# Token transform of batches 2 to 8: nine products become seven, and one table holds the issue order

## The chip, the cores and the metric

The kernel runs on one core of one Trainium2 chip. The metric is device time in microseconds (us). The kernel before takes 995.22 us, the median of three runs (994.12 to 995.35). The engines are PE (TensorE), DVE (VectorE), ACT (ScalarE), POOL (GpSimd) and SP (SyncE, here only an issuer of DMAs).

## The reference, cut to what matters

```
kv  = einsum('bhsd,bhse->bhde', k, v)          # 8 batches, 8 heads, 576 tokens, 64 wide
out = einsum('bhsd,bhde->bhse', q, kv)
x   = out / sqrt(mean(out*out, -1) + 1e-6) * g_norm   # then heads side by side: (8, 576, 512)
u   = x + real(fft(fft(x, axis=1), axis=2))
un  = (u - mean(u)) / sqrt(var(u) + 1e-6)
y   = u + relu(un @ w_ch1) @ w_ch2              # 512 -> 2048 -> 512
```

The Fourier transform over the 576 tokens is the "token transform" of the title; the one over the 512 channels is the "channel transform". Both are matrix products with cosine and sine tables.

## The kernel before, in words

The work is a list of small operations (`op`, `dma`), each with an engine, a cost, a rank, what it comes after and the buffers it holds. In the kernel before, `Plan.go` plays this list through on assumed costs and so finds an order; `MOVES` changes ranks, `SHIFTS` moves single operations in the finished line, and `settle` applies that. Every engine then executes its own instructions in the order in which they were emitted, and waits in place for what an instruction needs. SP's DMAs too are issued strictly in that order.

The code counts batches from 0, so "batches 2 to 8" are b = 1 to 7. For each batch: `plan_kv` (k'v, tile ps_k), `plan_q` (q transposed, ps_q), `plan_out` (q times kv, ps_o), `plan_y` (the root mean square), `plan_fold`, `plan_seq` (the token transform), `plan_chn` (the channel transform and the sum u), `plan_turn` (u transposed, split in two parts, into the blocks unTh and unTl for the feed-forward part). A product of two float32 matrices is made of three products of parts, high x high, high x low, low x high (`passes`), since each operand is kept as a high part and a low rest.

Fold and token transform: the symmetric halves of the 576 tokens are folded, which leaves 289 rows in three tiles t = 0, 1, 2 with 97, 96 and 96 rows. `plan_fold` makes the high part `xh` (ACT) and the rest `xl` (POOL or DVE) of each tile; in b = 1 to 7 the tiles come in the order 0, 1, 2. `plan_seq` then has four groups per batch (cosine or sine part, and two halves of the channels); a group sums nine products into one bank ps_f: three tiles times three passes, each 128 x 290 with 96 or 97 rows summed over (line 1532; b = 0 uses line 1544). The tables sit in `cs`, high and low, for three tiles. `p0_mm` (line 1964) does the same nine products once more for a single column of all batches.

The feed-forward part: NA = 3 of the 16 slices of the hidden layer are computed for a block of 512 tokens as soon as it is turned ("early", tiles ps_h and acc, lines 1012 and 1029), between the operations of the batches that follow. The remaining slices come after all batches. Line 1084 (`ps_s <- still`) emits products of a constant with itself whose result nobody reads ("spare" products); the plan puts them where PE has nothing ready.

What orders the work around the change: PE's and SP's own queues, in the emitted order; a fold needs `plan_y`'s result, a group of the token transform needs all three tiles' `xl`.

Of the kernel before, what the change touches and what calls it, by code (L numbers as in the profile page):

```python
# [9 lines left out]
F32 = mybir.dt.float32  # L10
# [4 lines left out]
ALU = mybir.AluOpType  # L15
# [61 lines left out]
SHIFTS = [  # L77
    ("plan_spare.go/PE/-/-", 20, 0),
    ("plan_w.<lambda>/DVE/w1/2", 3, -1),
    ("plan_w.<lambda>/DVE/w1/1", 1, -2),  # L80
    ("plan_q.take/ACT/3/11", 0, 2),
    ("plan_spare.go/PE/-/-", 18, 0),
    ("plan_spare.go/PE/-/-", 26, 0),
    ("plan_w.<lambda>/DVE/w2/2", 1, -4),
    ("plan_first_out.mean/DVE/0/1", 0, -2),
    ("plan_chn.<lambda>/DVE/1/1", 1, -6),
    ("plan_spare.go/PE/-/-", 31, 0),
    ("plan_first_out.square/ACT/0/2", 1, 9),
    ("plan_chn.<lambda>/ACT/1/2", 0, 5),
    ("plan_fold.even.go/DVE/1/1", 1, -2),  # L90
    ("plan_fold.fold/DVE/1/0", 0, -6),
    ("plan_spare.go/PE/-/-", 16, 0),
    ("plan_kv.<lambda>/POOL/2/-", 1, 9),
    ("plan_kv.<lambda>/POOL/5/-", 1, -2),
    ("plan_seq.<lambda>/PE/0/1", 0, -1),
    ("plan_turn.high/ACT/0/0", 0, -2),
    ("plan_out.red/DVE/2/1", 1, 10),
    ("plan_seq.<lambda>/PE/0/0", 1, 2),
    ("plan_q_load.load/SP/1/02", 0, 10),
    ("plan_spare.go/PE/-/-", 9, -4),  # L100
    ("plan_fold.mul/DVE/2/0", 0, -4),
    ("plan_q_load.<lambda>/SP/3/-", 0, 1),
    ("plan_spare.go/PE/-/-", 27, 0),
    ("plan_out.<lambda>/ACT/2/1", 0, -1),
    ("plan_kv.<lambda>/DVE/0/-", 0, 9),
    ("plan_fold.zero/ACT/1/1", 0, 4),
    ("plan_out.<lambda>/ACT/2/1", 1, 1),
    ("plan_first.<lambda>/PE/e0/-", 9, 3),
    ("plan_chn.put.<lambda>/SP/0/0", 1, 2),
    ("plan_kv.<lambda>/SP/1/-", 8, 1),  # L110
    ("plan_fold.zero/ACT/2/2", 0, -1),
    ("plan_chn.mix/DVE/0/0", 1, 5),
    ("plan_y.last/DVE/2/-", 0, -1),
    ("plan_seq.<lambda>/PE/0/0", 0, -2),
    ("plan_out.<lambda>/ACT/1/0", 1, 4),
    ("plan_kv.go/PE/1/-", 1, 1),
    ("plan_w.<lambda>/ACT/w2/0", 0, 9),
    ("plan_first.<lambda>/PE/e0/-", 4, 1),
    ("plan_first_out.mean/DVE/0/2", 0, 1),
    ("plan_first_out.mul/DVE/0/1", 0, 1),  # L120
    ("plan_early.<lambda>/ACT/e0/-", 3, -4),
    ("plan_out.scale/POOL/1/2", 0, 8),
    ("plan_chn.<lambda>/DVE/0/0", 0, 1),
    ("plan_kv.<lambda>/SP/5/-", 8, -2),
# [12 lines left out]
    ("plan_early.<lambda>/PE/e0/-", 10, -1),
    ("plan_out.scale/POOL/2/1", 1, 1),
    ("plan_spare.go/PE/-/-", 22, 0),
    ("plan_first_out.red/DVE/0/2", 1, -6),  # L140
    ("plan_fold.zero/ACT/1/2", 0, -2),
    ("plan_q.take/ACT/3/11", 0, -9),
    ("plan_w.<lambda>/DVE/w2/1", 1, 6),
    ("plan_first_out.red/DVE/0/2", 0, 1),
    ("plan_w.<lambda>/DVE/w2/0", 0, 9),
    ("plan_kv.<lambda>/SP/5/-", 7, 7),
    ("plan_w.<lambda>/DVE/w2/1", 0, 8),
    ("plan_first.<lambda>/DVE/e0/-", 1, -1),
    ("plan_spare.go/PE/-/-", 34, 0),
    ("plan_spare.go/PE/-/-", 33, 1),  # L150
    ("plan_chn.<lambda>/ACT/0/1", 0, 3),
    ("plan_q.turn/PE/4/01", 0, 9),
    ("plan_turn.turn/PE/0/1", 0, -2),
    ("plan_q.take/ACT/0/01", 0, -7),
    ("plan_chn.mm/PE/1/0", 1, 4),
    ("plan_turn.high/ACT/0/2", 1, -2),
    ("plan_chn.put.<lambda>/SP/0/0", 1, -2),
    ("plan_q_load.load/SP/1/-", 0, -1),
    ("plan_y.root/ACT/1/-", 0, 3),
    ("plan_w.<lambda>/DVE/w2/1", 5, -6),  # L160
    ("plan_spare.go/PE/-/-", 19, 0),
    ("plan_turn.low/DVE/0/1", 2, -1),
    ("plan_first.<lambda>/PE/e0/-", 0, -2),
    ("plan_turn.high/ACT/4/0", 2, 4),
    ("plan_out.red/DVE/2/1", 1, -3),
    ("plan_kv.<lambda>/POOL/3/-", 0, 1),
    ("plan_kv.<lambda>/ACT/6/-", 0, -2),
    ("plan_q.turn/PE/7/02", 0, 1),
    ("plan_chn.add_r/POOL/5/1", 0, -1),
    ("plan_early.<lambda>/ACT/e1/-", 7, 1),  # L170
    ("plan_y.recip/DVE/4/-", 0, -2),
    ("plan_early.<lambda>/ACT/e2/-", 5, -3),
    ("plan_fold.<lambda>/ACT/2/0", 0, -4),
    ("plan_turn.low/DVE/1/2", 0, 3),
    ("plan_out.red/DVE/6/2", 0, 1),
    ("plan_q.take/ACT/7/10", 0, 1),
    ("plan_first.<lambda>/PE/e2/-", 3, -1),
    ("plan_kv.<lambda>/SP/3/-", 9, -3),
    ("plan_out.mm/PE/3/2", 0, 6),
    ("plan_out.scale/POOL/4/2", 0, -3),  # L180
    ("plan_fold.<lambda>/ACT/3/1", 0, 9),
    ("plan_out.mm/PE/4/0", 0, 1),
    ("plan_chn.<lambda>/DVE/2/2", 1, 2),
    ("plan_chn.<lambda>/DVE/4/0", 0, 4),
    ("plan_first.<lambda>/PE/e3/-", 11, -6),
    ("plan_early.<lambda>/PE/e1/-", 7, -1),
    ("plan_early.<lambda>/ACT/e3/-", 3, -3),
    ("plan_out.og/ACT/6/1", 0, -7),
    ("plan_q.take/ACT/4/11", 0, -10),
    ("plan_turn.turn/PE/1/1", 0, 2),  # L190
    ("plan_seq.mm/PE/3/3", 0, 3),
    ("plan_chn.add_l/POOL/5/1", 0, 1),
    ("plan_seq.low/DVE/3/1", 0, -1),
    ("plan_q_load.load/SP/3/-", 0, 4),
    ("plan_kv.<lambda>/SP/4/-", 4, 2),
    ("plan_early.<lambda>/ACT/e1/-", 3, 1),
    ("plan_chn.<lambda>/DVE/0/0", 1, 9),
    ("plan_seq.mm/PE/3/0", 0, 2),
    ("plan_seq.mm/PE/3/2", 0, 3),
    ("plan_fold.<lambda>/ACT/3/1", 0, 4),  # L200
    ("plan_first.<lambda>/ACT/e3/-", 1, -1),
    ("plan_fold.low/DVE/1/1", 0, -1),
    ("plan_seq.<lambda>/ACT/2/1", 0, -2),
    ("plan_q.take/ACT/2/11", 0, -3),
    ("plan_turn.high/ACT/2/0", 3, 2),
    ("plan_turn.high/ACT/3/0", 3, 1),
    ("plan_chn.add_r/POOL/5/1", 0, -1),
    ("plan_out.<lambda>/ACT/6/0", 0, -2),
    ("plan_fold.<lambda>/ACT/1/1", 0, -4),
    ("plan_fold.low/DVE/2/2", 0, -2),  # L210
    ("plan_turn.low/DVE/1/1", 2, -1),
    ("plan_chn.<lambda>/DVE/3/2", 0, -3),
    ("plan_first.<lambda>/ACT/e2/-", 2, -2),
    ("plan_y.last/DVE/2/-", 0, -3),
    ("plan_kv.<lambda>/POOL/4/-", 1, 3),
    ("plan_seq.mm/PE/5/0", 0, 1),
    ("plan_turn.low/DVE/3/2", 0, -1),
    ("plan_out.og/ACT/5/2", 1, 3),
    ("plan_fold.<lambda>/ACT/1/1", 0, -2),
    ("plan_first.<lambda>/ACT/e2/-", 0, -1),  # L220
    ("plan_chn.mm/PE/5/2", 1, 2),
    ("plan_chn.mm/PE/5/2", 0, -4),
    ("plan_kv.go/PE/5/-", 1, -1),
    ("plan_turn.low/DVE/1/2", 2, -1),
    ("plan_turn.turn/PE/1/0", 1, 1),
    ("plan_chn.<lambda>/DVE/2/1", 0, 4),
    ("plan_fold.even.go/POOL/4/1", 1, -4),
    ("plan_fold.even.go/POOL/2/1", 1, -6),
    ("plan_fold.<lambda>/ACT/3/1", 0, -1),
    ("plan_out.red/DVE/4/1", 0, 6),  # L230
    ("plan_chn.mm/PE/3/0", 1, 9),
    ("plan_kv.<lambda>/POOL/4/-", 1, -2),
# [2292 lines left out]
```

## Time and profile before

| | |
|---|---|
| median of three timed runs | 995.22 us (994.12 to 995.35) |
| span of the profiled execution, first to last instruction | 993.5 us (its own device time is not listed apart from the span) |
| PE busy | 982.3 us, 99% |
| DVE, ACT, POOL busy | 690.1, 363.4, 397.6 us |
| DMA moved | 166.06 MB |
| PE in the first 60 us | 53.87 us busy |
| PE from 60 to 560 us | 499.9 us busy of 500 |

The profile counts an instruction as busy from its start to its modelled end. Neighbouring matmuls overlap, so the duration of one (some 300 to 400 ns) is longer than its share of PE's time; that share is read from a row of the chain of waits, where a merged piece gives the time of a whole run of products.

### The profile page before, as it was taken

The page shows a single profiled execution, that of the slowest core. Times are in us where ns is not written, and L with a number is a line of the kernel's source. Part 1 is how long each engine was busy: PE and PEld are TensorE (multiplying, and loading weights), DVE is VectorE, ACT ScalarE, POOL GpSimd, SP SyncE. Part 2 cuts the span into 40 slices and gives each one's busy share as a digit, 9 for nine tenths or more (in the row PEclk, how much of TensorE's full clock was granted, in tenths as well). Part 3 has the DMA queues.
Part 4 walks back from the last instruction along what each step waited for, and adds up shares of the span by engine and source line. Part 5 has one row for each costly group of instructions (what it writes and reads, how often), then busy time and mean ns, then how long its engine had stood idle before and what let it go on. Part 6 is the DMA issues. An engine that isn't in the chain of part 4 may idle for free.

```text
span 993.5 us, 17707 instructions
## 1 busy us (share of the span) xinstructions
PE 982.3 (99%) x6838; PEld 858.5 (86%) x6838; DVE 690.1 (69%) x1365; ACT 363.4 (37%) x731; POOL 397.6 (40%) x391
## 2 busy tenths in 40 slices
PE   8999999999999999999999999999999999999998
PEld 6888989988988888888888898989898888989897
DVE  4889886966667668767843786767676766767543
ACT  2466555655544333333332331323231313122221
POOL 1345443553554101434230372727272727263540
PEclk9899999999999999999999999999999999999999
DMA  9989797764453645565644515151525253424031
GB/s 231 236 222 271 210 275 230 200 161 165 144 195 117 267 168 192 181 252 211 225 170 159 201 44 212 44 212 53 202 81 187 100 171 115 153 107 149 1 127 43
DMA packets 111240, 166.06 MB, mean 167 GB/s; under 512 B 43710, under 2 KB 71666, under 8 KB 104756
## 3 DMA queue, kind: packets, MB, share of 16 engines
q1 hardware_dynamic: 103908, 149.06, 46.9%
q10 hardware_dynamic: 5328, 9.57, 2.6%
q0 software_dynamic: 1920, 6.29, 1.6%
q8 instruction: 54, 0.88, 0.4%
q14 instruction: 30, 0.25, 0.1%
HBM read 108.25 MB, written 56.64 MB: 166 GB/s over the span
## 4 chain that ended last, share of the span: by engine, by line
PE 94%; DMA 3%; SPq 1%; DVE 1%; issue 0%; ACT 0%; DVEq 0%; ACTq 0%
PE acc L1029 40%; PE ps_h L1012 20%; PE ps_h L2251 18%; PE ps_f L1586 4%; PE ps_f L1532 3%; PE ps_o L1304 3%; PE ps_k L1197 2%; PE ps_t L1684 2%; DMA vm<-in_v_dram 1%; PE ps_q L1279 1%; DMA draw<-in_dft_s_dram 1%; DMA qt<-in_q_dram 1%; PE ps_s L1084 1%; PE ps_o L1374 0%; SPq L1174 0%
## 5 line engine op out<-in xcount | busy, mean ns | idle before, releaser
L1029 PE MATMUL acc<-w,hh 128*128 128x512 f32 x1150 | 359.3, 394 | 0.0
L1029 PEld LDWEIGHTS acc<-w,hh 128*128 128x128 f32 x1150 | 205.7, 189 | 34.2
L1029 PE MATMUL acc<-w,hl 128*128 128x512 f32 x575 | 224.0, 390 | 0.0
L1021 ACT ACTIVATE hh<-ps_h 128x512 fp32r<-128x512 f32 x144 | 86.2, 598 | 345.8 <-DVE ps_h L2259 170.9
L1012 PE MATMUL ps_h<-unTh,w 128*128 128x512 f32 x576 | 179.3, 392 | 0.0
L1024 DVE SCALAR_TENSOR_TENSOR hl<-ps_h,hh 128x512 fp32r<-128x512 f32 x144 | 98.0, 684 | 92.1 <-ACT hh L1021 91.8
L1029 PEld LDWEIGHTS acc<-w,hl 128*128 128x128 f32 x575 | 108.0, 188 | 23.6
L1012 PEld LDWEIGHTS ps_h<-unTh,w 128*128 128x128 f32 x576 | 106.6, 188 | 21.3
L1012 PE MATMUL ps_h<-unTl,w 128*128 128x512 f32 x288 | 112.3, 390 | 0.0
L2211 POOL TENSOR_TENSOR up<-up 128x512 f32<-128x512 f32 x36 | 46.6, 1295 | 154.4 <-DMA up<-next_scr 119.2
L2259 DVE TENSOR_TENSOR ps_h<-part,ps_h 128x256 f32<-128x256 f32 x144 | 61.1, 425 | 40.9 <-ACT part L2264 23.3
L2259 DVE TENSOR_TENSOR part<-part,ps_h 128x256 f32<-128x256 f32 x108 | 45.4, 420 | 44.4 <-PE ps_h L2251 41.5
L1012 PEld LDWEIGHTS ps_h<-unTl,w 128*128 128x128 f32 x288 | 54.1, 188 | 11.5
L2224 POOL TENSOR_TENSOR uu<-uu,up 128x512 f32<-128x512 f32 x36 | 46.9, 1312 | 36.9 <-ACT up L2216 36.9
L1353 POOL TENSOR_TENSOR x<-x,gb 96x512 f32<-96x512 f32 (+1 forms) x26 | 33.8, 1311 | 45.0 <-ACT x L1320 45.0
L2264 ACT COPY part<-ps_h 128x256 f32<-128x256 f32 x36 | 13.4, 373 | 81.4 <-PE ps_h L2251 81.4
L1696 DVE TENSOR_TENSOR unTl<-ps_t,unTh 128x384 fp32r<-128x384 f32 (+13 forms) x80 | 34.0, 477 | 9.0 <-ACT unTh L1693 8.9
L2358 DVE SCALAR_TENSOR_TENSOR uu<-acc,bz,uu 128x512 f32<-128x512 f32 x35 | 25.0, 750 | 20.2 <-PE acc L1029 20.2
L1508 POOL TENSOR_TENSOR xe<-ab 96x256 f32<-96x256 f32 (+1 forms) x32 | 25.0, 797 | 34.0 <-DVE ab L1501 32.7
L1340 DVE TENSOR_REDUCE ss<-ps_o 96x8 f32<-96x512 f32 (+1 forms) x42 | 27.9, 682 | 14.1 <-ACT ps_o L1336 13.9
L1586 PE MATMUL ps_f<-cd,pt 128*96 128x258 f32 (+1 forms) x288 | 37.0, 283 | 0.0
L1586 PEld LDWEIGHTS ps_f<-cd,pt 128*96 128x96 f32 (+1 forms) x288 | 35.0, 162 | 1.3 <-DVE ss L1340 0.2
(226 smaller groups left out, 1875.9 us busy)
## 6 DMA issues: line engine op xcount, KB each, us to landing
raw<-in_moe_w_ch_dram SPq DMA_DIRECT2D x32, 512.0 KB, 3.9
unTh<-unT_scr SPq DMA_DIRECT2D x16, 1024.0 KB, 4.9
unTl<-unT_scr SPq DMA_DIRECT2D x16, 1024.0 KB, 7.3
qt<-in_q_dram SPq DMA_DIRECT2D x16, 576.0 KB, 6.7
unT_scr<-unTh SPq DMA_DIRECT2D x9, 1024.0 KB, 3.8
unT_scr<-unTl SPq DMA_DIRECT2D x9, 1024.0 KB, 7.3
part_scr<-part ACTq DMA_DIRECT2D x36, 256.0 KB, 4.0
next_scr<-part SPq DMA_DIRECT2D x36, 256.0 KB, 2.8
```

The costliest lines, as they stand in the source:

```text
L1012: nc.tensor.matmul(ps, w[c][:, kc * P : (kc + 1) * P], unT[a][:, kc, :], start=(kc == 0 and n == 0), stop=(kc == KC - 1 and n == 2),)
L1021: nc.scalar.activation(hh, ps, AF.Relu)
L1024: nc.vector.scalar_tensor_tensor(hl, ps, 0.0, hh.bitcast(F32), ALU.max, ALU.subtract)
L1029: nc.tensor.matmul(acc, hpair[a][:, i * P : (i + 1) * P], w[c], start=(first and n == 0), stop=(last and n == 2),)
L1304: nc.tensor.matmul(pss[s].t[:n, at : at + D], fqs[side].t[half, m, :n], kvt.t[half, m], start=True, stop=True,)
L1353: nc.gpsimd.tensor_tensor(v_, v_, gb[:n].unsqueeze(1).to_broadcast([n, H, D]), ALU.mult)
L1586: nc.tensor.matmul(ps.t[:n, :ND], pt.t[a][:, part, ch, offs[t] : offs[t] + n], cd[:, part, c, ch, :], start=(idx == 0), stop=(idx == 5),)
L1696: nc.vector.tensor_tensor(unTs[j].t[1][:, :, to], view()[:, :, lo:hi], unTs[j].t[0][:, :, to].bitcast(F32), ALU.subtract,)
L2211: lambda p=part: nc.gpsimd.tensor_tensor(p.t[:, 0], p.t[:, 0], p.t[:, 1], ALU.add),
L2224: lambda k=k, ut=ut, p=part: nc.gpsimd.tensor_tensor(ut.t[:, k], ut.t[:, k], p.t[:, 0], ALU.add),
L2251: nc.tensor.matmul(x(to), w.t[:, c, i, kk * P : (kk + 1) * P], rhs(a, kk), start=(kk == 0 and n == 0), stop=(kk == 1 and n == 2),)
L2259: return op("DVE", 415, URGENT, lambda: nc.vector.tensor_tensor(out(), a(), b(), ALU.add), d, bufs)
```

## The change: what it does

Three things are changed.

First, the 96 rows of tile 2 are given to others. Rows 36 to 63 (28 rows) are copied below the 97 rows of tile 0, rows 64 to 95 (32 rows) below the 96 rows of tile 1; those two tiles now have 125 and 128 rows. The 36 rows that are left are copied three times below each other, twice as high part and once as low part, into the place of `cs` that held the low table of tile 2, whose table in turn holds high, low and high. Their three passes are so one product over 108 rows. A group has 3 + 3 + 1 = 7 products. The copies are DMAs from SBUF to SBUF, issued on SP: five per batch for b = 1 to 7 (`plan_pack`), four for the tables once after b = 0 (`plan_basis`), six for the single column. Tile 2 is folded first in all batches, and a group waits for the five copies in place of tile 2's rest.

Second, `xh` and `xl` are now one tile `xhl`. The groups of b = 0 keep their nine products.

Third, `Plan.go`, `SHIFTS`, `MOVES` and `settle` are gone. A table of operation numbers (`ORDER`) is the order. Spare products that it does not name are not emitted: 10 are left of 54.

```diff
+ORDER = """
+5 242 385 212 208 209 234 226 227 210 221 211 218 397 219 213 222 216 215 386 4 387 388 389 390 391 392 239 393
...
     def run(self):
-        first = [o for o in self.ops if o.first]
...
+        line = [self.ops[int(n)] for n in ORDER.split()]
...
+        self.emit(line)
...
+    LEFT = 36
+    TO1 = TR, 2 * TR - P, P - TR
+    TO0 = TR + 1, LEFT, TO1[1] - LEFT
+    full = (TO0[0] + TO0[2], P)
+    AGAIN = (LEFT, 2 * LEFT)
...
+    def plan_pack(b, xs, dones):
+        r = rank(b, SEQ) - D2
+        out_ = []
+        for t, (at, lo, n) in enumerate((TO0, TO1)):
+            out_.append(dma(
+                4 * n, r, lambda t=t, at=at, lo=lo, n=n: move(xs[t].t[2][at : at + n], xs[2].t[2][lo : lo + n]),
+                [dones[2]], [xs[t], xs[2]],
+            ))
+        for a, at in ((0, 0), (0, AGAIN[0]), (1, AGAIN[1])):
+            out_.append(dma(
+                2 * LEFT, r, lambda a=a, at=at: move(cs[at : at + LEFT, :, 1, 2, :DH], xs[2].t[a][:LEFT]), [dones[2]] + basis + packed, [xs[2]],
+            ))
+        return out_
...
         def mm():
-            idx = 0
-            for t in range(3):
-                n = rows[t]
-                for a, c in passes:
+            for t in range(2):
+                for n, (a, c) in enumerate(passes):
                     nc.tensor.matmul(
                         ps.t[:, :NS],
-                        xs[t].t[a][:n, part, ch * P : (ch + 1) * P],
-                        cs[:n, part, c, t, :],
-                        start=(idx == 0),
-                        stop=(idx == 8),
+                        xs[t].t[a][: full[t], part, ch * P : (ch + 1) * P],
+                        cs[: full[t], part, c, t, :],
+                        start=(t == n == 0),
+                        stop=False,
                     )
-                    idx += 1
+            nc.tensor.matmul(
+                ps.t[:, :NS],
+                left_rows(part)[: 3 * LEFT, ch * P : (ch + 1) * P],
+                cs[: 3 * LEFT, part, 0, 2, :],
+                start=False,
+                stop=True,
+            )
...
-        for t in (2, 1, 0) if b == 0 else range(3):
+        for t in (2, 1, 0):
             plan.where = (b, t)
             xhl[t], lows[t], z = plan_fold(b, t, xs[t], y, yp, gs.get(t), muls.get(t))
...
+        if b:
+            packed = list(last_seq)
+            lows = lows[:2] + plan_pack(b, xhl, lows)
```

The next rows show what the table does to the order. On PE, the first group of the token transform of b = 1, before (ps_f is the bank that is summed into, a number tells buffers apart):

```order
L1029 MATMUL acc_1563<-w20_389,hl_1248 128x512
L1532 MATMUL ps_f_1573<-cs_108,xh_1381 128x290 x2
L1532 MATMUL ps_f_1573<-cs_108,xl_1382 128x290
L1532 MATMUL ps_f_1573<-cs_108,xh_1462 128x290 x2
L1532 MATMUL ps_f_1573<-cs_108,xl_1463 128x290
L1532 MATMUL ps_f_1573<-cs_108,xh_1481 128x290 x2
L1532 MATMUL ps_f_1573<-cs_108,xl_1482 128x290
```

and now, the first group and the start of the second:

```order
L704 MATMUL ps_k_1467<-vr_1405,kr_1342 64x64 x2
L1075 MATMUL ps_f_1515<-cs_108,xhl_1394 128x290 x3
L1075 MATMUL ps_f_1515<-cs_108,xhl_1402 128x290 x3
L1082 MATMUL ps_f_1515<-cs_108 128x290
L1075 MATMUL ps_f_1525<-cs_108,xhl_1394 128x290 x3
```

A group has six products of the two filled tiles and one of the stacked rows, each as wide as before.

On SP, the DMAs around the five copies of b = 1 (xhl<-xhl and cs<-xhl), which did not exist before:

```order
L976 DMA xhl<-xhl 28x1024
L671 DMA vm<-in_v_dram 128x2x256
L671 DMA km<-in_k_dram 128x2x256
L976 DMA cs<-xhl 36x2x256
L681 DMA kr<-in_k_dram 64x4x64
L976 DMA xhl<-xhl 32x1024
L681 DMA kr<-in_k_dram 64x4x64
L681 DMA vr<-in_v_dram 64x4x64 x2
L976 DMA cs<-xhl 36x2x256
L671 DMA vm<-in_v_dram 128x2x256
L976 DMA cs<-xhl 36x2x256
```

Seven loads of a later batch stand between the first copy and the last one. In b = 2 the five stand one behind the other.

At the start of PE's queue, before (ps_s are the spare products):

```order
L1084 MATMUL ps_s<-still 128x512 x18
L1273 MATMUL ps_q<-ident,qt 64x96 x8
L1273 MATMUL ps_q<-ident,qt 64x97 x8
L970 MATMUL ps_w<-wa,mean_t 128x128 x4
L1273 MATMUL ps_q<-ident,qt 64x96 x8
L1084 MATMUL ps_s<-still 128x512 x2
L1273 MATMUL ps_q<-ident,qt 64x96 x24
```

and now:

```order
L780 MATMUL ps_q<-ident,qt 64x96 x8
L472 MATMUL ps_w<-wa,mean_t 128x128 x4
L591 MATMUL ps_s<-still 128x512 x2
L780 MATMUL ps_q<-ident,qt 64x96 x8
L780 MATMUL ps_q<-ident,qt 64x97 x8
L780 MATMUL ps_q<-ident,qt 64x96 x8
L591 MATMUL ps_s<-still 128x512 x4
```

The 18 spare products ahead of the first transposes are gone, as are most of the others. Ahead of the first feed-forward product (line 1012 before) stood 48 of them and stand 10 now, and four transposes of q fewer; the other products ahead of it are the same ones in another order.

## Rows read from the trace of the kernel before

**Rows 1.** The page, busy time, share and instructions of each engine.
```profile
PE 982.3 (99%) x6838; PEld 858.5 (86%) x6838; DVE 690.1 (69%) x1365; ACT 363.4 (37%) x731; POOL 397.6 (40%) x391
```

**Rows 2.** Stretches: length, each engine's busy us, granted clock, DMA share, GB/s.
```profile
0.00:60.00 60.00, 53.87 (x748) 45.91 (x750) 39.48 (x75) 25.07 (x52) 16.85 (x29) 0.94 0.97 236
60.00:210.00 150.00, 149.91 (x1666) 134.21 (x1664) 127.65 (x268) 89.48 (x210) 71.20 (x95) 1.00 0.83 235
210.00:320.00 110.00, 110.00 (x768) 96.26 (x765) 71.11 (x143) 55.06 (x126) 52.26 (x58) 1.00 0.41 144
```

**Rows 3.** Chain that ended last: start, length, what; startup to early feed-forward.
```profile
19.16 1.60 PE ps_s L1084 x6
...
21.36 10.62 DMA draw<-in_dft_s_dram
...
37.58 2.00 PE ps_s L1084 x4
...
43.26 1.14 PE ps_s L1084 x4
...
54.63 3.90 DMA vm<-in_v_dram
...
72.35 0.62 DVE unTl L1696
...
78.88 0.89 PE ps_h L1012 x3
79.78 0.93 PE ps_s L1084 x4
80.70 7.48 PE ps_h L1012 x33
```

**Rows 4.** The same chain: token transform of b = 1, p0, and a piece through DVE.
```profile
101.23 4.85 PE ps_f L1532 x36
...
297.93 1.19 PE ps_o L1964 x9
...
568.68 0.43 DVE ps_h L2259
...
570.91 0.17 DVE bz L2113
```

**Rows 5.** Instructions that write ps_f: count, shortest, median, longest ns, first and last start.
```profile
L1532 PE MATMUL ps_f<-cs,xh x168: 293/297/400, 101.1 to 308.6; 96*128 96x290 f32 x112, 97*128 97x290 f32 x56
L1532 PE MATMUL ps_f<-cs,xl x84: 289/296/303, 101.3 to 308.7; 96*128 96x290 f32 x56, 97*128 97x290 f32 x28
```

**Rows 6.** The same for ps_s, all, and those from 62 us on.
```profile
L1084 PE MATMUL ps_s<-still x54: 389/400/793, 1.7 to 255.3; 128*128 128x512 f32 x54
...
L1084 PE MATMUL ps_s<-still x8: 389/393/477, 69.6 to 255.3; 128*128 128x512 f32 x8
```

**Rows 7.** PE alone, stretches around 34 us: length, busy, granted clock, DMA share, GB/s.
```profile
30.00:34.00 4.00, 2.61 (x46) 1.00 1.04 266
34.00:42.00 8.00, 8.00 (x92) 0.57 1.16 219
```

**Rows 8.** Longest waits of PE in total: total us, times, longest.
```profile
PE ps_s L1084 <- DVE still L1076: 1.7, 1, 1.7
PE ps_k L1197 <- DMA vm<-in_v_dram: 1.3, 3, 0.9
```

**Rows 9.** POOL in order of time, the rests of the three tiles of b = 6.
```profile
251.77 1.74 POOL L1517 TENSOR_TENSOR xl<-xe,xh 97x512 fp32r<-97x512 f32 x1 [1.07 <-ACT xh L1514]
...
259.67 1.28 POOL L1517 TENSOR_TENSOR xl<-xe,xh 96x512 fp32r<-96x512 f32 x1 [1.35 <-ACT xh L1514]
```

**Rows 10.** DMA issues: count, KB each, median us from issue to landing.
```profile
kr<-in_k_dram SPq DMA_DIRECT2D x16, 64.0 KB, 4.9
...
u_scr<-x SPq DMA_DIRECT2D x8, 30.0 KB, 4.3
...
unT_scr<-unTl SPq DMA_DIRECT2D x9, 1024.0 KB, 7.3
```

**Rows 11.** SP in order of time: start, length of the issue.
```profile
101.26 0.60 SPq L1240 DMA_DIRECT2D qt<-in_q_dram  x1
...
106.53 0.47 SPq L1164 DMA_DIRECT2D km<-in_k_dram  x1
```

More of the change, by code (lines that the diff above doesn't have):

```diff
@@ L566 @@
+ORDER = """
[182 rows of a table added]
+"""
 class Buf:
@@ L604, in __init__ @@
         self.ops = []
-        self.now = 0
         self.where = ("-", "-")
@@ L615, in op @@
         o.key = (f"{what}/{b}", f"{what}/{b}/{t}")
-        o.rank = rank + sum(MOVES.get(k, 0) for k in o.key)
         o.after = [a for a in after if a is not None]
@@ L796, in settle @@
-    def settle(self, line):
-        named = {}
-        for o in self.ops:
-            named.setdefault(o.key[1], []).append(o)
-        for key, k, n in SHIFTS:
-            o = named[key][k]
-            if o not in line:
-                continue
-            if not n:
-                line.remove(o)
-                continue
-            step = 1 if n > 0 else -1
-            at = i = to = line.index(o)
-            while n:
-                i += step
-                if not 0 <= i < len(line) or o in line[i].after or line[i] in o.after:
-                    break
-                if line[i].eng == o.eng:
-                    n -= step
-                    to = i
-            line.insert(to, line.pop(at))
-        return line
+        seen = set()
@@ L819, in emit @@
+        line = [self.ops[int(n)] for n in ORDER.split()]
+        for o in line:
+            seen.add(o.n)
+            if any(a.n not in seen for a in o.after):
+                raise RuntimeError(f"{o.key} stands ahead of what it needs")
+        self.emit(line)
     def emit(self, line):
@@ L1462, in plan_y, with xhl_tile, move, left_rows @@
         return op("DVE", 200, r, last, [c], [ss, yp], port=True), yp
+    def xhl_tile():
+        both = one.tile([P, 2, 2, DH], F32R, name="xhl", tag="xhl", bufs=RINGS["xhl"])
+        return [both[:, 0], both[:, 1], both]
+    def move(dst, src):
+        nc.sync.dma_start(dst.bitcast(F32), src.bitcast(F32))
+    def left_rows(part):
+        return cs[:, part, 1, 2, :DH]
+    def plan_basis(after):
+        def copy(dst, src):
+            return dma(150, rank(0, SEQ), lambda: move(dst, src), after)
+        out_ = []
+        for t, (at, lo, n) in enumerate((TO0, TO1)):
+            out_.append(copy(cs[at : at + n, :, :, t], cs[lo : lo + n, :, :, 2]))
+        for c, at in zip((1, 0), AGAIN):
+            out_.append(dma(
+                80, rank(0, SEQ),
+                lambda c=c, at=at: move(cs[at : at + LEFT, :, 0, 2], cs[:LEFT, :, c, 2]),
+                after + out_[:2],
+            ))
+        return out_
+    def plan_pack(b, xs, dones):
+        r = rank(b, SEQ) - D2
+        out_ = []
+        for t, (at, lo, n) in enumerate((TO0, TO1)):
+            out_.append(dma(
[3 more added lines that the diff above has]
+        for a, at in ((0, 0), (0, AGAIN[0]), (1, AGAIN[1])):
+            out_.append(dma(
+                2 * LEFT, r, lambda a=a, at=at: move(cs[at : at + LEFT, :, 1, 2, :DH], xs[2].t[a][:LEFT]), [dones[2]] + basis + packed, [xs[2]],
+            ))
+        return out_
     def plan_fold(b, t, x, y_done, yp, gs, ms=None):
@@ L1473, in plan_fold @@
             ab, xe = e2_buf("ab"), e2_buf("xe")
-        xhl = Buf("xhl", lambda: [
-            one.tile([P, 2, DH], F32R, name=c, tag=c, bufs=RINGS["xhl"]) for c in ("xh", "xl")
-        ])
+        xhl = Buf("xhl", xhl_tile)
         def xv(s):
@@ L1560, in plan_seq @@
             a = a[0]
+            last_seq.append(a)
         else:
-            a = op("PE", 1200, r, mm, dones + [dft["s", part]], [ps, pt] + xs)
+            a = op("PE", 940, r, mm, dones + [dft["s", part]], [ps, pt] + xs)
+            last_seq.append(a)
         h = op(
@@ L1928 @@
         xhl, lows = [None] * 3, [None] * 3
-        for t in (2, 1, 0) if b == 0 else range(3):
+        for t in (2, 1, 0):
             plan.where = (b, t)
@@ L1935 @@
         pts = []
+        plan.where = (b, "-")
+        if b:
+            packed = list(last_seq)
+            lows = lows[:2] + plan_pack(b, xhl, lows)
+        last_seq.clear()
         for grp in range(4):
@@ L1938 @@
             pts.append(plan_seq(b, grp, xhl, pt, lows))
+        if not b:
+            plan.where = (b, "-")
+            basis += plan_basis([dft["s", part] for part in range(2)] + last_seq)
         for t in (2, 1, 0) if b == 0 else range(3):
@@ L1955, in p0_in @@
     def p0_in():
-        nc.vector.tensor_copy(x0h, x0)
-        nc.vector.tensor_tensor(x0l, x0, x0h.bitcast(F32), ALU.subtract)
+        nc.vector.tensor_copy(x0h[: TR + 1], x0)
+        nc.vector.tensor_tensor(x0l[: TR + 1], x0, x0h[: TR + 1].bitcast(F32), ALU.subtract)
     def p0_mm():
-        idx = 0
-        for t in range(3):
-            n = rows[t]
-            for a, c in passes:
+        for t in range(2):
+            for n, (a, c) in enumerate(passes):
                 nc.tensor.matmul(
-                    ps0.t[:B, :NS],
-                    (x0h, x0l)[a][:n, t, :],
-                    cs[:n, 0, c, t, :],
-                    start=(idx == 0),
-                    stop=(idx == 8),
-                )
-                idx += 1
+                    ps0.t[:B, :NS], (x0h, x0l)[a][: full[t], t, :], cs[: full[t], 0, c, t, :],
+                    start=(t == n == 0), stop=False,
+                )
+        nc.tensor.matmul(
+            ps0.t[:B, :NS], x0h[: 3 * LEFT, 2, :], cs[: 3 * LEFT, 0, 0, 2, :], start=False, stop=True
+        )
     def p0_out():
@@ L1982 @@
     a = op("DVE", 300, r, p0_in, zeros)
-    a = op("PE", 1200, r, p0_mm, [a], [ps0])
+    d = [a]
+    for t, (at, lo, n) in enumerate((TO0, TO1)):
+        for x_ in (x0h, x0l):
+            d.append(dma(
+                1, r, lambda t=t, at=at, lo=lo, n=n, x_=x_: move(x_[at : at + n, t], x_[lo : lo + n, 2]), [a],
+            ))
+    for at, x_ in zip(AGAIN, (x0h, x0l)):
+        d.append(dma(
+            1, r, lambda at=at, x_=x_: move(x0h[at : at + LEFT, 2], x_[:LEFT, 2]), d[:5],
+        ))
+    a = op("PE", 1000, r, p0_mm, d + basis, [ps0])
     a = op("DVE", 900, r, p0_out, [a], [ps0, p0t, p0u])
```

668 lines of the change are left out of this document (6 added, 662 removed), and 181 rows, old and new, of the table ORDER.

## The prediction

> **What bounds the kernel now.** I read the page first: PE is busy for 982.3 of the 993.5 us of the span, DVE for 690.1, the rest for less than half [rows 1]. The reader is to see there that only PE can be the bound over the whole, and that the other engines matter only where they make PE wait. Then the stretches: PE is busy for 149.91 of 150 us from 60 to 210 us and for all 110 from 210 to 320, at full clock, while DMA is at 0.83 in the first of these and 0.41 in the second; DVE, the next one, has 127.65 of 150 us, 85% [rows 2]. Only the first 60 us look different: PE 53.87 of 60, DMA at 0.97. The chain of waits says the same in order of time: up to 78.88 us it goes through DMA landings, spare products and DVE steps, and from the first feed-forward product on it is PE alone [rows 3], but for 2.4 us between 568.68 and 571.08 us, where it passes through DVE [rows 4], in a part that the change leaves as it is. PE's longest waits by cause are 1.7 and 1.3 us, and both lie in the start [rows 8]. So a product that is taken out after 79 us should come off the end one for one, as long as the others keep up, and one taken out before that may not.
>
> A busy PE is not proof that each product costs its duration. A token-transform product lasts 297 ns in the median [rows 5], but 36 of them take 4.85 us in the chain [rows 4], 135 ns each. That is the price to use: the longer number counts overlap twice.
>
> **The change part by part.**
>
> *Fewer products.* Before, lines 1532 make 168 + 84 = 252 products, 36 for each of seven batches [rows 5]. The order now shows 6 + 1 per group, 28 per batch, 196: 56 fewer. 56 x 135 ns = 7.55 us, all of it later than 101 us, where the chain is PE. That 97 rows become 125 and 96 become 128 or 108 I cost at nothing: rows with 96 and 97 rows summed over show the same 293 ns at least and 296 to 297 in the median [rows 5], and the 290 columns that set it stay. It could not be less than nothing, and if the duration grew with the rows by their ratio 128/96, the 28 remaining products would cost as much as 36 did and the gain would be gone; nothing in the rows points that way.
>
> *The single column.* 9 products of line 1964 take 1.19 us [rows 4], 132 ns each; two fewer, 0.26 us. Its six tiny copies are issued after the last fold and PE has feed-forward products around it; 0.
>
> *Spare products.* 54 [rows 6] become 10 in the order. Most stand in the start, where their going changes nothing directly. From 62 us on there were 8 [rows 6] and the order keeps two of these. Four took 0.93 us in the chain at 79.78 us [rows 3], 0.23 each: 6 x 0.23 = 1.4 us off.
>
> *The start.* Ahead of the first feed-forward product the orders hold the same real products but four transposes, so PE's load there is the same; when it ends is set by what data arrive and by DVE. Three spare pieces lie on the chain, 1.60, 2.00 and 1.14 us, 4.7 together [rows 3], which is the most that their removal can give. Behind the first and the third the chain goes on with a DMA landing, the table loads (10.62 us) and a load of v (3.90 us) [rows 3], so these two would only uncover that. Of the middle one, which stands between real products, I take half, 1.0 us. The other end is a loss: in 30 to 34 us PE was busy for only 2.61 of 4 us, and in the 8 us that followed the clock was 0.57 in the mean, which cost 8 x 0.43 = 3.4 us of PE [rows 7]. Without spares there may be two such stretches more on the path, 6.8 us. The start thus is between -4.7 and +6.8; I take -1.0.
>
> The Trainium skill, "TensorE: Matmul & The Clock Gate", Part 1 (The HAM clock gate), says that half clock is the array's default and that activity is what lifts it; taking idle-time products out would by that rule cost in the start. Rows 7 agree with the fall after idle time. The first 18 spares, which would have paid for the lift, are those that go, and by the rule alone the start would come out at the upper end of its range.
>
> *The copies.* SBUF to SBUF copies are not in the trace. The nearest rows are loads of 64 KB, 4.9 us to landing, and stores of 30 KB, 4.3 us [rows 10]; these copies have 72 to 128 KB. Each issue holds SP for about 0.5 to 0.6 us [rows 11], five for 3 us. Copies can start when tile 2's rest is made. That is now first: in b = 6 the first rest ended at 253.51 and the last at 260.95 [rows 9], so 7.4 us of folding cover 3 + 4.9 = 7.9 us of copying. That is 0.5 us late per batch, and 3.5 us over seven, if PE had nothing else to do. In b = 1 seven loads of 1,024 KB in all stand between the copies; at 235 GB/s [rows 2] they take 4.4 us, so 9.3 us stand against 7.4. But PE's queue was not waiting for the rest before: no such row is among its waits [rows 8], so the group stands some way behind its data. What this slack is cannot be read. I take 1.0 us in all. The lower end is 0; the upper is 3 + 7.3 us (the slowest landing of rows 10) - 7.4 = 2.9 us per batch, 20 us.
>
> The Trainium skill, "DMA: Bandwidth & Descriptors", Anatomy of one DMA, puts the fixed part of a DMA (measured on GpSimd's path) at about 2.0 us. With 128 KB at its rate, some 2.3 us by that page as an estimate, the five copies would be covered and the term would be 0. The rows, taken while other transfers are under way, are longer, and they go into the sum.
>
> *Traffic and queue.* 456 KB x 7 = 3.2 MB of copies come to the 166 MB. Between 60 and 210 us that is about 4 batches, 1.8 MB at 235 GB/s or 8 us of 150 at most, 0.83 becomes 0.88; no wait is added while loads are issued this far ahead. What is queued behind a copy that waits for tile 2's rest is SP's next load; PE is its victim one batch later. Cost 0, part of the upper end above.
>
> *DVE as cover.* It does the same work in a part that is 7.6 us shorter; 127.65 of some 145 us is 88%. It stays below PE.
>
> *The sum.* 993.5 - 7.55 - 0.26 - 1.4 - 1.0 + 1.0 = 984.3 us of span. The median of the timed runs lies 995.22 - 993.5 = 1.7 us above the span; with that, 986.0 us, 0.9% less than before.
>
> **The rivals.**
>
> *Late copies (slower).* SP issues strictly in order, so the five copies block loads while they wait, and the loads block copies while they land; the groups of the token transform come late, PE stands, and the next batch's loads come late too. For it speaks that the copies of b = 1 are spread among seven loads and that DMA is at 0.83 there [rows 2]. Against it speaks the cover of 7.4 us and feed-forward products before many groups. At 2.9 us per batch it costs 20 us in place of 1.0: 986.0 + 19 = 1005. It decides the sign from (995.2 - 985.0) / 7 = 1.5 us per batch on. Chance 0.10; half as bad, 2 to 10 us given back, is within the range.
>
> *Half clock in the start.* With 38 spares fewer ahead of the first feed-forward product, PE's own work becomes the bound of the start. Three stretches like that at 34 us are 10.2 us, against -1.0: 986.0 + 11 = 997. For it speaks [rows 7]; against it, that real products follow closely in the new order and lift the clock again as they did at 42 us, and that data, not PE, end most pieces of the chain there. Chance 0.09.
>
> *A better start.* The order of the start is wholly new. If the spare pieces on the chain do fall away, and a little of the waits on DMA with them, 4.7 to 7 us go in place of 1.0: 980 to 982. DVE's 39.48 of 60 us [rows 2] would allow it; that the same bytes must come in at 236 GB/s speaks against it. Chance 0.15.
>
> *The gain is hidden.* If DVE or DMA set the pace from 60 to 210 us, the four transforms there would give nothing, about 4.3 us of the 7.55: 990. Their shares, 85% and 0.83, speak against it. Chance 0.08. That the products are not really fewer is excluded by the order.
>
> **How the numbers follow.** My forecast has 0.58 and ends between 983 and 990. About 0.2%, 2 us, is what a measurement of this kernel can tell from no change. Faster by more: forecast 0.58, better start 0.15, hidden gain 0.08, and a few hundredths of the rivals that are less bad: 0.84. Within: 0.06. Slower: 0.10, the two slow rivals at their price. The range goes from 979 (the better start) to 995 (the point where late copies or the clock have eaten all).
>
> **What the profile will show.** Right: 196 products in the two new lines with 28 per batch in about 3.8 us; the chain PE alone from about 78 us; every feed-forward step after 320 us some 9 us earlier, with the same spacing. Wrong: waits of PE's token-transform products on a DMA of `xhl` or `cs`; a first feed-forward product later than 82 us, with the clock at 0.50 for more than 8 us of the start; SP waits before the copies followed by PE waits on k, v or q; a product of 128 rows that takes more than 135 ns.

## The result, and the profile after

The changed kernel takes 1000.83 us (median of 4 runs, 999.57 to 1004.68) against 995.29 for the kernel before on the same chip: ratio 1.0061, 95% interval 1.0045 to 1.0076. It is 0.6% slower. The forecast was 986.0 us, faster, with a range of 979 to 995: the sign and the range are both wrong. The profiled execution of the kernel after is the slowest of its four (1004.68 us), so its profile shows some 4 us more than the median.

The page of the kernel after, to set beside [rows 1]:
```profile
PE 970.8 (97%) x6736; PEld 845.6 (84%) x6736; DVE 683.0 (68%) x1365; ACT 357.8 (36%) x731; POOL 395.3 (39%) x391
```
PE is busy for 11.5 us less, and the span is 1002.7 in place of 993.5: its idle time has grown from 11.2 to 31.9 us. The stretches of [rows 2], after (length, busy us of each engine, granted clock, DMA share, GB/s):
```profile
0.00:60.00 60.00, 46.58 (x726) 42.81 (x727) 37.90 (x78) 25.24 (x53) 17.40 (x29) 0.89 0.86 215
60.00:210.00 150.00, 142.57 (x1546) 125.95 (x1545) 120.73 (x251) 82.69 (x198) 64.94 (x90) 0.98 0.83 231
210.00:320.00 110.00, 107.91 (x774) 91.64 (x773) 73.79 (x150) 56.71 (x130) 53.56 (x60) 1.00 0.54 175
```
The first row looks bad and is not where the time went: 10 us of its idle is the first wait for `qt`, where spare products ran before, and the first feed-forward product starts 1.7 us earlier than before. PE in order of time, before and after:
```profile
78.81 0.73 PE L1012 MATMUL ps_h<-unTh,w 128*128 128x512 f32 x2
```
```profile
77.13 0.71 PE L514 MATMUL ps_h<-unTh,w 128*128 128x512 f32 x2
```
Most of the loss is in the second row: from 60 to 210 us PE was busy for all but 0.09 us before, and now it stands for 7.43 us and runs part of the rest at half clock. From the first feed-forward product to the first product on a pair of tiles it is 489.2 us now (77.13 to 566.35) and was 481.9 (78.81 to 560.70), where 9.2 us fewer had been forecast. An estimate, added up over stretches of 0.5 us, closes the account: PE's busy time there, counted at full clock, fell from 481.9 to 473.7 us, about as forecast; 12.5 us of idle and 3.1 us lost to the clock came on top.

PE's waits in the whole span, largest first (total us, times, longest):
```profile
PE ps_q L780 <- DMA qt<-in_q_dram: 12.0, 2, 10.2
PE ps_b L1701 <- DVE dg L1693: 3.0, 1, 3.0
PE ps_o L811 <- ACT fq L790: 2.4, 1, 2.4
PE ps_f L1082 <- DMA cs<-xhl: 1.4, 1, 1.4
PE ps_q L786 <- DVE ss L847: 1.4, 1, 1.4
```
No single releaser has the loss. Two rows are of the kind that the prediction had named: `cs<-xhl`, a copy of tile 2, once, 1.4 us; and, too small for this list, 0.6 us for a copy of the column sums. The others name no copy. That does not clear the copies: the second wait for `qt` (1.2 us, at 134.89 us) is absent in the run below that has this order without them. The 3.0 us of `ps_b` lie at 539 us, far behind the last copy; the same wait is 0 to 1.3 us in the other profiles of this order.

The products themselves came out as priced (count, shortest, median, longest ns, first and last start):
```profile
L1075 PE MATMUL ps_f<-cs,xhl x168: 289/297/403, 101.9 to 307.6; 125*128 125x290 f32 x84, 128*128 128x290 f32 x84
L1082 PE MATMUL ps_f<-cs x28: 293/297/373, 102.8 to 307.8; 108*128 108x290 f32 x28
```
196 products, and 125, 128 and 108 rows have the median, 297 ns, that 96 and 97 had in [rows 5] (296 to 297).

**One gap, followed back.** The 2.39 us wait for `fq` lies at 108 us. ScalarE in order of time (start, length, work, and in brackets how long it stood before and for what):
```profile
98.19 0.57 ACT L1420 COPY part<-acc 128x512 f32<-128x512 f32 x1
100.69 0.59 ACT L1420 COPY part<-acc 128x512 f32<-128x512 f32 x1 [1.93 <-PE acc L531]
101.30 1.75 ACTq L1424 DMA_DIRECT2D part_scr<-part  x2
...
107.40 0.59 ACT L1420 COPY part<-acc 128x512 f32<-128x512 f32 x1 [2.72 <-DMA part_scr<-part]
107.89 0.49 ACT L790 COPY fq<-ps_q 128x384 f32<-128x384 f32 x1
```
A finished accumulator is copied to one of two `part` slots and stored from there by ScalarE's own queue. The third copy needs the first slot back; the stores of the first two go out together at 101.30 us, and that landing is in the chain of waits as "101.30 6.08 DMA part_scr<-part". ScalarE stands until 107.40, and `fq`, for which PE waits, stands behind the copy. In the kernel before, the copies at the same place began at 95.74, 99.13 and 110.24 us, each with its store right behind it. Over 60 to 400 us ScalarE's wait for these stores is 17.7 us in 8 places; it was 3.3 in 3. In the run of this order without copies the same gap of PE is 1.6 us (at 107.51 us), so most of it is the order's. What followed on PE:
```profile
107.90:114.70 6.80, 6.27 (x77) 6.04 (x78) 4.11 (x8) 2.78 (x8) 2.23 (x5) 0.50 0.87 258
```
PE was busy at clock 1.00 until the gap began at 106.04 us; at its end the clock is at its lower level, and stays there for over 6 us. Half of the 6.27 us in which PE is busy, 3.1 us, is lost. The gap costs more behind it than in it.

### The profile page after: what moved, and what is told of

Its sections match the earlier page's. It is cut to its first block, busy times and chain, and to the rows that moved or that the text cites. A ratio compares the mean times of both kernels' runs of the same rounds, so it can differ in the third digit from the quotient of the medians.

```text
span 1002.7 us, 17541 instructions
## 1 busy us (share of the span) xinstructions
PE 970.8 (97%) x6736; PEld 845.6 (84%) x6736; DVE 683.0 (68%) x1365; ACT 357.8 (36%) x731; POOL 395.3 (39%) x391
## 4 chain that ended last, share of the span: by engine, by line
PE 80%; DMA 10%; DVE 4%; issue 2%; ACT 2%; POOL 1%; SPq 1%; ACTq 0%; DVEq 0%; POOLq 0%
PE acc L531 34%; PE ps_h L1818 18%; PE ps_h L514 13%; DMA part_scr<-part 4%; PE ps_f L1137 3%; PE ps_o L811 3%; DMA qt<-in_q_dram 2%; PE ps_k L704 2%; DMA raw<-in_moe_w_ch_dram 2%; PE ps_t L1235 1%; PE ps_f L1075 1%; PE ps_q L780 1%; PE ps_q L786 1%; DMA uu<-u_scr,rowidx 1%; PE ps_o L881 1%
## 5 line engine op out<-in xcount | busy, mean ns | idle before, releaser
L1247 DVE TENSOR_TENSOR unTl<-ps_t,unTh 128x384 fp32r<-128x384 f32 (+14 forms) x80 | 34.8, 474 | 17.8 <-ACT unTh L1244 17.8
L1137 PE MATMUL ps_f<-cd,pt 128*96 128x258 f32 (+1 forms) x288 | 41.4, 289 | 0.8 <-DVE pt L1120 0.8
L448 DVE TENSOR_SCALAR ps_a<-ps_a 128x512 f32<-128x512 f32 x32 | 22.1, 695 | 28.7 <-ACT ps_a L441 28.5
L1244 ACT ACTIVATE unTh<-ps_t 128x384 fp32r<-128x384 f32 (+15 forms) x80 | 33.5, 493 | 17.5 <-PE ps_t L1235 15.6
```

The lines of the kernel that those rows point to most:

```text
L1137: nc.tensor.matmul(ps.t[:n, :ND], pt.t[a][:, part, ch, offs[t] : offs[t] + n], cd[:, part, c, ch, :], start=(idx == 0), stop=(idx == 5),)
L1244: nc.scalar.activation(unTs[j].t[0][:, :, to], view()[:, :, lo:hi], AF.Copy)
L1247: nc.vector.tensor_tensor(unTs[j].t[1][:, :, to], view()[:, :, lo:hi], unTs[j].t[0][:, :, to].bitcast(F32), ALU.subtract,)
```

## The experiments

Each ratio is against the kernel before, run on the same chip in the same rounds, with its 95% interval.

### Order, products and copies apart

Three kernels undo parts of the change. The first is the kernel before with two passes fewer for the third tile (the result lacks them); the same is done for the single column:
```diff
-                for a, c in passes:
+                for a, c in passes if t < 2 else passes[:1]:
```


> The kernel before with its own order, row for row, but 7 products per group: of tile 2 only the product high x high is made, the other two are left out, and nothing is copied; the single column likewise. Theory A (the products come off as priced, and what the kernel after lost it lost by its new issue order): 56 x 0.135 + 0.26 = 7.8 us less than before, 987 to 988. Theory B (the products were never worth 7.8 us, since the other engines set the pace of the first part): 992 to 995. Theory C (the copies did the harm): 987 to 988, as A.

989.63 us, 0.9929 (0.9914 to 0.9944): -7.1 us, of the 7.8 that the 58 products were priced at. In the old order the products come off the end; theory B is out.

The second has the searched order, nine products, and no copies (`move` is empty).

> The kernel after with its table of the issue order, but nine products per group of tiles of 97, 96 and 96 rows and no copies; the operations of the copies are empty. Theory A (the new order costs some 14 us): about 7 us more than the kernel after, 1004 to 1010, if its stalls do not hide the products, and 1000 to 1004 if they hide half of them. Theory C (the copies cost it): the copies' waits go, the products come back, 993 to 998.

1007.50 us, 1.0105 (1.0088 to 1.0123). The order costs 10.5 us without the rest, and theory C (the copies did the harm) is out. The order is counted here with what comes along with it: 44 spare products fewer, tile 2 folded first, and the merged tile `xhl`. No run sets these apart; the merged tile is also in the last kernel below, which is faster than the kernel before.

The third has the searched order, seven products and no copies.

> The kernel after with its table of the issue order and 7 products, but no copies: of tile 2 only high x high is made, the other two products are left out. Against the kernel after it takes away the copies alone. Theory A: 1.4 to 3 us less than the kernel after (its one wait on a copy of the token transform is 1.4 us, the one of the single column 0.65), 998 to 1000. Theory C: 10 us less or more, 985 to 991.

997.84 us, 1.0015 (1.0000 to 1.0029). From the second to the third, seven products for nine are worth 9.0 us (1.0105 - 1.0015); from the third to the changed kernel, the copies cost 4.6 (1.0061 - 1.0015; 3.3 by the medians, and some 2 us either way by the intervals). 10.5 - 9.0 + 4.6 = 6.1: the three steps lead from the kernel before to the changed one, so they add up to its 1.0061 by themselves.

A fourth kernel, the changed computation with the old planner in place of the table, gave no time: on the new list of operations that planner finds no slot of `qt` for a load of q. What the old planner would have made of the change stays open.

### What the order's price is made of

In the run of the order alone the largest loss is at 220 us. ScalarE, then PE, in order of time:
```profile
218.62 0.60 ACT L1059 ACTIVATE xhl<-ps_xe 96x512 fp32r<-96x512 f32 x1
223.81 0.59 ACT L1413 COPY part<-acc 128x512 f32<-128x512 f32 x1 [4.59 <-DMA part_scr<-part]
...
224.80 1.06 ACT L843 ACTIVATE ps_o<-ps_o 96x512 f32<-96x512 f32 x2 [0.40 <-ACT part L1413]
```
```profile
226.72 0.87 PE L1228 MATMUL ps_t<-ident,x 96*128 96x96 f32 x4 [3.92 <-DVE ss L847]
...
230.71 7.61 PE L1075 MATMUL ps_f<-cs,xhl 97*128 97x290 f32 x36 [1.98 <-ACT xhl L1059]
```
The squares (L843) stand 4.59 us behind the blocked copy, DVE's sums behind the squares, and PE behind the sums. The releaser that PE's row names, DVE, is two steps from the cause. To take that wait away, 9 of the copies go to another ring that has a slot free there:
```diff
-            part = Buf("part", part_tile)
+            part = early_part(j, i)   # the ring "e2" for (j, i) in a list of 9
```


> The searched order with nine products and no copies (+10.5 us by its own run, 1007.5) with the one edit of the run part_in_e2: 9 copies of finished accumulators go to the other ring. Theory A (the order's price is ScalarE standing in place for the store of a finished accumulator: 4.59 us at 219.2 us, TensorE's idle 3.92 and 1.98 us behind it, then clock 0.91 over 200 to 260 us): 1000 to 1003 us, and the stretch of 200 to 300 us busy again for 98 us or more (it was 93.9). Rival B (the order is tight everywhere and the next operand is as late): 1006 to 1009 us, with other releasers in TensorE's waits.

1002.48 us, 1.0071 (1.0049 to 1.0093), 3.4 us less by the ratios, 5.0 by the medians (the intervals overlap by 0.0005), in A's band. From 200 to 300 us, before and after this edit (A wanted 98 us busy):
```profile
200.00:300.00 100.00, 93.86 (x730) 80.60 (x729) 59.21 (x118) 47.88 (x111) 46.30 (x56) 0.95 0.45 147
```
```profile
200.00:300.00 100.00, 97.35 (x761) 83.51 (x760) 62.71 (x122) 49.17 (x114) 51.61 (x61) 0.98 0.45 147
```
In that run ScalarE's wait for the stores falls from 16.0 us to 7.5. The same edit in the changed kernel:

> The changed kernel with one edit: 9 of the first 24 copies of a finished accumulator go to a slot of another ring of the same size (that of the folded tiles, which has a slot free there), so ScalarE's next copy does not stand in place for the store of the one before. Theory A (the searched order puts these copies where their ring is still being stored, ScalarE waits 17.7 us for that in 60 to 400 us, and TensorE's operands behind it come late, then its clock falls): most of the 17.7 us goes, the 2.39 us gap at 108 us and the half clock behind it (about 3.5 us) go, 992 to 996 us. Rival B (the order is too tight on several engines, and the next releaser takes its place): 999 to 1002 us, ScalarE's waits move to TensorE's accumulators.

998.84 us, 1.0029 (1.0011 to 1.0047): 2.0 us less by the medians, 3.2 by the ratios (the intervals overlap by 0.0002), at B's edge rather than in A's band. ScalarE's wait for the stores fell from 17.7 to 7.4 us, and the 2.4 us wait of `ps_o` for `fq` is gone (another, of `ps_q`, is 0.8 us), but a wait for `km`, absent before, is 2.8. Both theories hold a part: about 4 of the order's 10.5 us are this ring of two, and in this kernel another operand was then as late. ScalarE's waits for feed-forward results over 60 to 400 us (the kernel before, then the run of the order alone):
```profile
ACT hh L1021 <- PE ps_h L1012: 57.3, 30, 4.9
```
```profile
ACT hh L523 <- PE ps_h L514: 26.0, 16, 4.2
```
This wait is less than half as long as in the old order. All of ScalarE's waits for PE together fell less, from 125.7 to 109.0 us, so a smaller lead of ScalarE would fit and is not shown. I have not taken the other 6 us apart.

### What the copies cost

Here every instruction of the kernel before keeps its place and the change's products and copies are put in (the merged tile too).

> The change's seven products with all its copies, but every other instruction in the order of the kernel before; each copy stands 12 rows behind the last step of the third tile, which is the last to be folded in six of the seven batches. Theory A (order and copies are two separate prices; here the order costs nothing, but a copy takes 4 to 8 us to land and its tile is ready only some 8 to 30 rows ahead of the product): TensorE waits 1 to 4 us in most batches, 994 to 1006 us against 989.6 without the copies. Rival B (other work of TensorE hides them): 989 to 992 us.

1034.51 us, 1.0391 (1.0365 to 1.0417), some 45 us above the run without copies and far beyond what A allowed. PE's waits over 60 to 570 us, and the longest of them:
```profile
PE ps_f L1092 <- DMA xhl<-xhl: 19.0, 5, 8.3
PE ps_f L1099 <- DMA cs<-xhl: 8.5, 6, 2.1
```
```profile
110.69 1.79 PE L1092 MATMUL ps_f<-cs,xhl 125*128 125x290 f32 x6 [8.26 <-DMA xhl<-xhl]
```
A landing in the chain takes 2.37 to 2.81 us after 200 us ("242.84 2.81 DMA cs<-xhl") and 7.70 us at 102.86, where the DMA engines are full. Over 60 to 320 us PE is busy for 235.73 us at clock 0.95. Then the third tile takes the first-folded tile's place:

> As the run before it, with the third tile taking the place of the first-folded tile in the order of batches 2 to 8 (its transposes, products, norms and fold change places with that tile's), so the copies start 29 to 70 rows ahead of the product. Theory A (late landing is the copies' only price): 988 to 991 us, faster than both kernels. Rival C (the copies' traffic and their places in the queue of SyncE cost 3 to 4 us wherever they stand, as between the two runs of the searched order): 992 to 995 us.

1007.58 us, 1.0115 (1.0096 to 1.0135): A was wrong, and C's band is missed as well. No product of the token transform waits for a copy any more. PE waits over 60 to 570 us for loads of v, and 5.1 us for the copies of the column sums (`x0h`, `x0l`):
```profile
PE ps_k L721 <- DMA vr<-in_v_dram: 3.0, 1, 3.0
PE ps_o L1543 <- DMA x0h<-x0l: 2.7, 1, 2.7
PE ps_k L721 <- DMA vm<-in_v_dram: 2.0, 3, 1.4
PE ps_o L1539 <- DMA x0h<-x0h: 1.8, 1, 1.8
```
The 3.0 us are paid at batch 2. PE, then SyncE's queue ahead of it (start, length), then the same place in the kernel before:
```profile
101.91 0.34 PE L721 MATMUL ps_k<-vr,kr 128*64 128x64 f32 x4 [3.02 <-DMA vr<-in_v_dram]
```
```profile
90.72 1.32 SPq L698 DMA_DIRECT2D kr<-in_k_dram  x2
92.28 1.58 SPq L993 DMA_DIRECT2D xhl<-xhl  x2
93.91 2.60 SPq L993 DMA_DIRECT2D cs<-xhl  x3
96.56 0.66 SPq L698 DMA_DIRECT2D vr<-in_v_dram  x1
```
```profile
92.45 0.61 SPq L1174 DMA_DIRECT2D vr<-in_v_dram  x1
```
Issuing five copies takes SyncE 4.2 us, and the load of v goes out 4.1 us later. At the copies of batch 3 the queue stands as well (the first row ends at 109.66):
```profile
109.19 0.47 SPq L688 DMA_DIRECT2D km<-in_k_dram  x1
113.28 1.58 SPq L993 DMA_DIRECT2D xhl<-xhl  x2
114.96 3.38 SPq L993 DMA_DIRECT2D cs<-xhl  x3
118.44 1.37 SPq L698 DMA_DIRECT2D kr<-in_k_dram  x2
```
SyncE stands 3.6 us for the tile's rest, issues for 5.0 us, and the loads of k and v start 8.8 us after the queue was free (4.9 us in the kernel before, whose queue stands there too). This time PE did not pay: it has no wait above 0.3 us from 103 to 144 us. Is it the place or the traffic?

> The kernel of the run old_order_copies_first with each of its copies of the tables and of batches 2 to 8 cut to one row (those of the eight column sums stay whole), the products reading the rows that are there: the same instructions at the same places in SyncE's queue, 3.7 MB less traffic; the third tile's low-order products are left out of the result by this. Theory Q (the copies cost by their places in SyncE's queue, ahead of loads, and by the column sums' two copies in a row): 1004 to 1008 us. Theory T (they cost by traffic and by the time of landing): 991 to 997 us, of which about 5 to 8 us are the column sums' wait.

1011.78 us, 1.0167 (1.0146 to 1.0188), slower than with whole copies and outside both bands. But the edit changed the products too: the product of the stacked rows runs over 37 rows in place of 108, and it lasts longer. Whole copies, then one-row copies, each with a piece of the chain:
```profile
L1099 PE MATMUL ps_f<-cs x28: 292/298/374, 106.7 to 316.9; 108*128 108x290 f32 x28
314.35 0.80 PE ps_f L1092 x6
315.15 0.14 PE ps_f L1099
```
```profile
L1099 PE MATMUL ps_f<-cs x28: 394/395/400, 106.5 to 322.6; 37*128 37x290 f32 x28
318.98 1.00 PE ps_f L1092 x6
319.98 0.33 PE ps_f L1099
```
A group of seven takes 1.33 us there in place of 0.94. From the first feed-forward product to the first pair of tiles, PE's busy time counted at full clock is 484.0 us against 476.0 (an estimate over stretches of 0.5 us), so about 8 us of this run belong to its products. What PE lost there to idle time and clock is 11.8 us, against 15.0 with whole copies. So most of the price goes with the number of the copies and their places, as Q said, and some 3 us may go with their bytes.

> The kernel of the run old_order_copies_first with only places in the order changed: the copies of batches 2 and 3 go 20 rows further back in SyncE's queue, behind the loads of k and v that came late (TensorE waited 5.0 us for them), and the product with the column sums, with what follows it, goes behind the products of batch 8 (TensorE waited 5.1 us for its copies and ran at clock 0.83 over 300 to 320 us). If those waits are the whole difference to the run without copies (989.6): 989 to 993 us, faster than both kernels. If the copies' traffic delays the loads wherever they stand: 996 to 1002 us.

1003.53 us, 1.0079 (1.0061 to 1.0097): 4 us better than with the copies first, and neither forecast. The wait for `vr` at 102 us is gone, but a copy now came 3.9 us late (`xhl<-xhl`), clock 0.83 followed over 100 to 120 us, and the later column sums left a wait of 2.3 us. In batches 2 and 3, neither of the two places tried is both early enough for the product and late enough for the loads.

> The order of the kernel before, with nine products in batches 1 to 3 and seven, with the copies, in batches 4 to 8 only; in those the third tile takes the place of the first-folded one, the tables' copies go out behind batch 3's products, and the column sums' product goes behind batch 8's. It saves 40 x 135 ns = 5.4 us of products. Theory Q (a copy costs where SyncE's queue and the DMA engines are full, which is up to 160 us: 6.8 us of TensorE's idle lay between 100 and 160 us in the run old_order_copies_first, none between 160 and 300): 989.5 to 993 us, faster than both kernels. Rival (any copy set costs its 2 to 3 us, the seven products never pay): 996 to 1003 us.

993.97 us, 0.9984 (0.9973 to 0.9994): faster than both kernels, than the one before by 1.7 us of the 5.4 saved, and 1 us above Q's band. (Of the 6.8 us of idle that Q names, the waits in that run show 4.8.) The largest of PE's waits; none is for a copy:
```profile
PE ps_k L721 <- DMA vm<-in_v_dram: 1.8, 2, 0.9
PE ps_s L608 <- DVE still L600: 1.7, 1, 1.7
PE ps_f L1102 <- DVE unTl L1274: 1.4, 1, 1.4
PE ps_q L797 <- DMA qt<-in_q_dram: 1.3, 2, 1.1
PE ps_f L1102 <- DVE ss L864: 1.2, 1, 1.2
```
The two waits of `ps_f` belong to batches 4 and 5, where the tile that is now folded last is late.

## Why the prediction was wrong

- **The step that failed** is the condition in "a product that is taken out after 79 us should come off the end one for one, as long as the others keep up". The products did come off (-7.1 and -9.0 us); the others did not keep up in the new order. The sum had terms for what the order loses (spares) and for the start, and none for the order of 80 to 400 us itself. It took PE's gap-free stretches [rows 2] as a property of the work, when they were one of that order. With the table the instructions of every engine stand in a new order, so waits that had been hidden could come out. Forecast and result lie 15.3 us apart (9.2 less, 6.1 more). By the ratios, 12.9 of these are the order, which cost 10.5 where -2.4 stood for spares and start; 3.6 are the copies; the products gave 1.2 back. No rival named the order.
- **Fewer products, -7.55, and the single column, -0.26:** right. -7.1 us in the old order, -9.0 in the searched one; 108 to 128 rows did not lengthen a product.
- **Spares, -1.4:** 10 spares are left as read; in time this term can't be told from the order's price.
- **The start, -1.0:** right in sign and near in size, -1.7 us. It was a choice between -4.7 and +6.8, so luck has a part in it. The rival of half clock came true in its condition and not in its price. After 1.83 us of idle the rows are
```profile
30.00:40.00 10.00, 8.89 (x90) 8.35 (x90) 7.83 (x17) 4.42 (x9) 3.64 (x5) 0.50 0.94 220
40.00:50.00 10.00, 10.00 (x199) 9.58 (x198) 5.98 (x13) 3.94 (x9) 4.77 (x6) 0.85 0.64 196
```
  so 4.4 + 1.5 = 5.9 us of PE's busy time were lost to the clock, where the kernel before lost 3.4 [rows 7]. The start still became shorter; that data and DVE set its end, as in [rows 3], would fit this, and no run tests it. The Trainium skill, "TensorE: Matmul & The Clock Gate", Part 1 (The HAM clock gate), has half clock as the state that activity must lift: these rows agree with that, and the time that it would have made of the start did not appear.
- **The copies, +1.0 (0 to 20):** 4.6 us, inside the bounds and on the wrong side of the value taken. Two of its parts were off: an issue was put at 0.5 to 0.6 us and took 0.6 to 0.9, up to 1.8, and landings in the chain of the run old_order_copies went from 2.1 to 7.7 us, not 4.9. The Trainium skill, "DMA: Bandwidth & Descriptors", Anatomy of one DMA, with its fixed part of about 2.0 us (for GpSimd's path) agrees with the shortest only.
- **Traffic and queue, 0:** wrong. "No wait is added while loads are issued this far ahead" fails in the run old_order_copies_first: five issues put the load of v 4.1 us back, and PE waits 3.0 us for it. The delay at batch 3 was longer and cost PE nothing, so a late load alone does not give the price.
- **Late copies** did not decide the sign in the changed kernel (1.4 us on PE at batch 3), but where the fold order gave no cover they cost 6.4 us a batch (45 / 7). The rival's 2.9 was worked out with 7.4 us of cover; without cover the prediction's own 3 + 4.9 = 7.9 us a batch lie above what was measured, so this run does not show the rival's price to be too low.
- **Hidden gain:** excluded by the run in the old order. **DVE as cover, 0:** the late operands that come through DVE trace back, in the case followed at 220 us, to ScalarE; no run shows DVE as the bound.

## What to carry to other kernels

When a change brings a new issue order, price the order by itself: for each ring with few slots, read from both orders how far apart its users stand and set that against the landing time of the transfer that frees the slot. A wait in an in-order queue is paid by whatever stands behind it, so read the next instruction on that engine, and then whether PE waits for it; the releaser that PE names can be two steps from the cause. A transfer that waits for a computed tile belongs behind the loads in its queue, or in a stretch where the queue has room; taking the gain only there (batches 4 to 8) made the one version that computes the whole result and beat both kernels. And a run that thins out one cost must leave the others as they were: the one-row copies had to be set against 8 us of slower products.

## What the runs showed of the hardware that I had not expected

- A gap of 2.39 us was followed by 3.1 us lost to the clock. In the run of the order alone, PE stood for 6.1 us between 222 and 231 us (3.92 and 1.98 us shown above, 0.2 between them), and from 226 to 236 us it had half clock:
```profile
226.00:236.00 10.00, 7.07 (x29) 6.29 (x30) 6.86 (x12) 3.76 (x8) 1.27 (x1) 0.50 0.01 2
```
  Half of the 7.07 us, 3.5 us, are lost on top, so 9.7 us in one place, two thirds of the 14.2 us that this run lost to idle time and clock between the first feed-forward product and the first pair of tiles (an estimate over stretches of 0.5 us).
- A product over 37 rows, between products over 97 and 98 rows, lasted 395 ns in the median, where one over 108 rows lasted 298 ns, and the six products behind it took 1.00 us in place of 0.80.
